# Block 0's last tile turned by a DMA on ScalarE's queue, and V of its second half made one tile at a time

## The chip, the cores and the metric

The kernel runs on one core of a Trainium2 chip. Its engines are named as the profile names them: PE (TensorE: matmuls, with PEld for its weight loads), DVE (VectorE), ACT (ScalarE), POOL (GpSimd) and SP (SyncE), which issues most DMAs; ACT has a DMA queue of its own. The metric is the device time of one execution in microseconds (us), and the plain runs are reported by their median. One more execution is taken with the hardware profiler; durations come from that one.

## The reference

Four layers work on x, 2048 tokens by 1024 columns in bf16: attention, a gated two-matrix feed-forward, and both once more with the same weights.

```python
x = A_x
x = x + _A_ref(_layernorm(x, axis=-1), A_wqkv, A_wo)
x = x + _B_ref(_layernorm(x, axis=-1), B_W_gate, B_W_up, B_W_down)
x = x + _A_ref(_layernorm(x, axis=-1), A_wqkv, A_wo)
x = x + _B_ref(_layernorm(x, axis=-1), B_W_gate, B_W_up, B_W_down)
```

`_A_ref` multiplies the normalized x with `wqkv` to Q, K and V in 32 heads of 32 columns; each token attends to itself and seven tokens 2, 4, ... 14 places earlier; the result is multiplied with `wo`. `_B_ref` is `(relu(x @ W_gate) * (x @ W_up)) @ W_down` with 3584 columns inside. `_layernorm` takes the mean off each row and divides by the root of the variance plus 1e-5.

## The kernel before

The tokens are cut into four blocks of 512 (`BLK`), and a block into four tiles of 128 rows. Eight passes (two pairs of layers times four blocks) are laid out by hand as a list of events with due times; `emit` sorts them, and so the order of the instructions on each engine is fixed. Helpers chain what they issue: `mm` and `pe_group` for PE, `dv` for DVE, `sp_dma` (line 115; the DMA issue itself is line 118 or 121) for SP's queue, and `on` (line 323) inside the first normalization for DVE, ACT ("a") and POOL ("g"). Line 132 is any matmul, line 423 a transpose on PE, line 106 any chained DVE operation, line 328 an operation of `on`.

This case is about the first 30 us, in which block 0 is normalized and multiplied with V's weights. A matmul wants the normalized x with its columns on the partitions, so every tile has to be turned: `xnT[:, t, kc, :]` is the chunk kc (of eight, 128 columns each) of tile t. In `ln_first` PE turns a tile by eight transposes into PSUM (`turn`, line 411), and ACT or DVE copies the two halves of four chunks into `xnT` (`copy`, line 426). Later blocks are turned by a DMA transpose on SP's queue.

Tiles 0 and 1 are turned without their scale, to start sooner; V of these two is scaled by `scaled(i)` (line 487) as DVE takes it out of PSUM, and `widen` (line 399) scales their part of `xnT` afterwards for Q and K. Tiles 2 and 3 are normalized fully by `apply` (line 404) before they are turned. Tile 3's statistics come from ACT (`square_of`, `act_mean`), tile 2's from DVE.

V's weights come in two slabs of four chunks each, `("v0", 0)` and `("v0", 1)`, loaded chunk by chunk in `load_slab` (line 222) with the loads of x's tiles 2 and 3 among them. V of a block has eight column groups c, and a PSUM bank (`pairs[part, c // 2]`) holds two of them for two tiles. `prod(kc, c, t0, t1)` (line 476) is one matmul of chunk kc, group c, tiles t0 to t1: 128 columns for one tile, 256 for two. `halves(i, part, k0)` (line 496) does both groups of a bank from chunk k0 on, for both tiles of the part. The order of all this is that of `head` (line 501).

Weights lie in a ring of five slabs (`RING`, line 58). The slab after the fifth, the second half of K's weights, goes into the buffer of V's first slab, so SP waits at it until PE has read that slab for the last time; behind it on SP's queue stand tiles of x for later blocks, a small zero pad of V's store, and block 1's four transposes.

```python
if (t, c) == (2, KC // 2):
    later(3)
    ln["widen"]()
```

These lines stand in `head` in the middle of tile 2's matmuls: `later(3)` turns and copies tile 3 there. After the four-chunk matmuls of tiles 2 and 3, `halves` finishes both tiles together, chunks 4 to 7.

Of the kernel before, what the change touches and what calls it, by code (L numbers as in the profile page):

```python
# [13 lines left out]
P = 128  # L14
D = 1024
# [5 lines left out]
KC = D // P  # L21
BLK = 512
TPB = BLK // P
# [8 lines left out]
def _ap(t, off, dims):  # L32
    return bass.AP(tensor=t.tensor, offset=t.offset + off, ap=[list(t.ap[0])] + [list(d) for d in dims])
# [3 lines left out]
def kernel(  # L37
# [11 lines left out]
    nc = tc.nc  # L49
# [51 lines left out]
    def dv(f, *args, **kwargs):  # L101
        if tail_dve[0] is None:
            tail_dve[0] = f(*args, **kwargs).ins
        else:
            with tc.issue_after(tail_dve[0]):
                tail_dve[0] = f(*args, **kwargs).ins  # L106
# [8 lines left out]
    def sp_dma(dst, src, transpose=False):  # L115
        start = nc.sync.dma_start_transpose if transpose else nc.sync.dma_start
        if tail_sp[0] is None:
            tail_sp[0] = start(dst, src).ins  # L118
        else:
            with tc.issue_after(tail_sp[0]):  # L120
                tail_sp[0] = start(dst, src).ins  # L121

    @contextmanager
    def pe_group():
        if tail_pe[0] is None:
            yield
        else:
            with tc.issue_after(tail_pe[0]):
                yield

    def mm(*args, **kwargs):
        tail_pe[0] = nc.tensor.matmul(*args, **kwargs).ins  # L132

    def big_tile(shape, name, early=False):
        where = pool["early"] if early else big
        return where.tile(shape, BF16, tag="big", name=name)
# [34 lines left out]
    def load_x(b, tiles=range(TPB)):  # L171
        for t in (b * TPB + i for i in tiles):
            if t == 0:
                sp_dma(x_tiles[t][:, 0:SLAB], x_dram[t * P:(t + 1) * P, 0:SLAB])
                nc.scalar.dma_start(x_tiles[t][:, SLAB:D], x_dram[t * P:(t + 1) * P, SLAB:D])
            elif t == 1:
                nc.scalar.dma_start(x_tiles[t][:], x_dram[t * P:(t + 1) * P, :])
            else:
                sp_dma(x_tiles[t][:], x_dram[t * P:(t + 1) * P, :])
# [42 lines left out]
    def load_slab(key, src):  # L222
        shp = list(src.shape)
        t = wring.tile([P, 8 * SLAB], BF16, tag="slab", name="w_" + "_".join(str(k) for k in key))
        tv = t[:, 0:shp[1] * shp[2]].rearrange("p (a b) -> p a b", b=shp[2])
        if key[0] == "v0":
            for i, (k0, k1) in enumerate(((0, 1), (1, 2), (2, 3), (3, 4)) if key[1] == 0 else ((0, 1), (1, 2), (2, 3), (3, 4))):
                if (key[1], i) in ((1, 1), (1, 2)):
                    load_x(0, [i + 1])
                sp_dma(tv[:, k0:k1, :], src[:, k0:k1, :])  # L230
        else:
            sp_dma(tv, src)
        slab[key] = tv
# [59 lines left out]
    def ln_dve_stats(xt):  # L293
# [9 lines left out]
        return mv, rstd  # L303

    load_slab(("v0", 0), qkv_half(2, 0))
    load_slab(("v0", 1), qkv_half(2, 1))
    load_slab(("qk01", "q", 0), qkv_half(0, 0))

# [8 lines left out]

    def ln_first():
        hold = {"xnT": xnT_pool.tile([P, TPB, KC, P], BF16, tag="xnT", name="xnT_first")}
        xna = big_tile([P, TPB, D], "xn_first", True)  # L320
        last = {}

        def on(eng, f, *args, **kwargs):
# [148 lines left out]
    def v_first(ln):  # L472
        st = att[0]
        pairs, opened = {}, set()

        def prod(kc, c, t0, t1):
            part = t0 // 2
            if (part, c // 2) not in pairs:
                pairs[part, c // 2] = psum.tile([P, 2, BLK // 2], F32, tag="acc", name="acc_v")
            acc = pairs[part, c // 2][:, c % 2, (t0 % 2) * P:(t0 % 2 + t1 - t0) * P]  # L480
            with pe_group():
                mm(acc, lhsT=slab["v0", kc // (KC // 2)][:, kc % (KC // 2), c * P:(c + 1) * P],
                   rhs=ln["xnT"][:, t0:t1, kc, :], start=(part, c // 2) not in opened, stop=(kc == KC - 1),
                   skip_group_check=True)
            opened.add((part, c // 2))

        def scaled(i):
            dv(nc.vector.tensor_tensor, st["vT"][:, 2 * i:2 * i + 2, 0:2 * P], pairs[0, i][:],
               _ap(ln["rb"], 0, [[0, 2], [1, 2 * P]]), op=ALU.mult)

        def later(t):
            ln["turn"](t)
            ln["copy"](t, "a", 0)
            ln["copy"](t, "a", 1)

        def halves(i, part, k0):
            for c in (2 * i, 2 * i + 1):
                for kc in range(k0, KC):
                    prod(kc, c, 2 * part, 2 * part + 2)

        def head():
            st["vT"] = big_tile([P, KC, BLK], "vT_0", True)
            ln["open_up"]()

            def chunk(kc, t):
                for c in range(KC):
                    prod(kc, c, t, t + 1)

            for kc in range(3):
                chunk(kc, 0)  # L510
            ln["turn"](1, (0,))
            ln["copy"](1, "v", 0)
            chunk(3, 0)
            ln["turn"](1, (1,))
            ln["copy"](1, "a", 1)
            ln["spread_rstd"]()
            for kc in range(4):
                chunk(kc, 1)
            chunk(4, 0)
            chunk(4, 1)  # L520
            ln["bn"](2, 0)
            ln["bn"](2, 1)
            ln["aggr"](2)
            ln["apply"](2)
            sq = ln["square_of"](x_tiles[3][:])
            ln["act_mean"](3)
            ln["act_power"](3, sq)
            chunk(5, 0)
            chunk(5, 1)
            for c in range(4):  # L530
                prod(6, c, 0, 2)
            for i in range(KC // 2):
                if i == 2:
                    later(2)
                halves(i, 0, 7 if i < 2 else 6)
                if i == 2:
                    ln["apply"](3)
                scaled(i)
            for t in (2, 3):
                for c in range(KC):  # L540
                    if (t, c) == (2, KC // 2):
                        later(3)
                        ln["widen"]()
                    for kc in range(KC // 2):
                        prod(kc, c, t, t + 1)
            for i in range(KC // 2):
                halves(i, 1, KC // 2)
                ln["on"]("a", nc.scalar.copy, st["vT"][:, 2 * i:2 * i + 2, 2 * P:BLK], pairs[1, i][:])
            tail_act[0] = ln["last"]["a"]

        return head
# [279 lines left out]
    def gu_steps(n, ln):  # L831
        hold = {}

        rs, ups = {}, {}

        def mults(j):
            def f():
                if j == 0:
                    hold["hT"] = pool["hid"].tile([P, FC, BLK], BF16, tag="hT", name=f"hT_{n}")
                s4, jl = j // 4, j % 4  # L840
                for nm in ("g", "u"):
                    acc = psum.tile([P, BLK], F32, tag="acc", name=f"acc_{nm}")
                    with pe_group():
                        for kc in range(KC):
                            mm(acc[:], lhsT=slab[(nm, n, s4)][:, kc, jl * P:(jl + 1) * P], rhs=ln["xnT"][:, :, kc, :],
                               start=(kc == 0), stop=(kc == KC - 1))
                    if nm == "g":
                        rs[j] = pool["hid"].tile([P, BLK], BF16, tag="r", name="r", bufs=3)
                        with tc.issue_after(tail_exp[0]):
                            tail_act[0] = nc.scalar.activation(rs[j][:], acc[:], ACT.Relu).ins  # L850
                    else:
                        ups[j] = acc
            return f

        def gate(j):
            def f():
                dv(nc.vector.tensor_tensor, hold["hT"][:, j, :], ups.pop(j)[:], rs.pop(j)[:], op=ALU.mult)
            return f

        return ([(2 * GRP * j, mults(j)) for j in range(FC)] + [(2 * GRP * (j + 1) - 0.05, gate(j)) for j in range(FC)],  # L860
                hold)
# [88 lines left out]
    ln_a = {}  # L950
    ln_b = {}
    ln_a[0] = ln_first()

    def zero_v():
# [36 lines left out]
    want_qk("qk23", t_qk2 + GRP * 2 * KC, t_gu0)  # L991
    want_wo(0, t_fill, t_fill)
    head = v_first(ln_a[0])
    ev.append((0.25, head))
    ev.append((0.35, lambda: load_x(1, [0, 1])))
# [53 lines left out]
    for n in range(NN):  # L1049
        gu, hold = gu_steps(n, ln_b[n])  # L1050
# [103 lines left out]
```

## Time and profile before

| | |
|---|---|
| median of three plain runs | 1616.0 us (1615.85 to 1616.05) |
| profiled execution | 1619.0 us, span 1617.3 us |
| PE busy | 1609.1 us, 99% of the span |
| DVE, ACT, POOL busy | 71%, 29%, 11% |
| PE from V's first long stretch (8.6 us) to Q's first matmul (25.0 us) | one chain without a hole |
| K weights, second half | issued at 21.56 us, after a wait of 9.6 us |

In the rows of a timeline the first column is the start in us from the span's start, the second the length; "x8" says that eight instructions of one kind are put together, and square brackets give idle time of the engine before the row and what ended it. In the chain of waits the second column is the time that the piece holds the chain. Matmuls overlap in their ends, so the length of one matmul is no price of it; prices are taken from chains of many.

### The profile page before, as it was taken

What the parts mean: (1) busy time and instruction counts of PE and PEld (TensorE: products, weight loads), DVE (VectorE), ACT (ScalarE), POOL (GpSimd) and SP (SyncE); (2) the same over time, 40 slices, a digit from 0 to 9 for tenths busy, and PEclk for the clock granted to TensorE, in tenths of its full rate; (3) what the DMA queues carried; (4) which work ended last, traced back from release to release, by engine and by line L of the source; (5) the groups of instructions that cost most, each with busy time, mean ns of one, the idle gap of its engine ahead of it and who ended that gap; (6) DMA issues with size and microseconds to landing.
All of it is one profiled execution on the core that took longest, in us unless ns stands there. A gap on an engine that the chain in (4) does not pass through costs nothing.

```text
span 1617.3 us, 19041 instructions
## 1 busy us (share of the span) xinstructions
PE 1609.1 (99%) x7651; PEld 790.5 (49%) x7701; DVE 1141.6 (71%) x969; ACT 474.8 (29%) x968; POOL 175.3 (11%) x174
## 2 busy tenths in 40 slices
PE   9999999999999999999999999999999999999999
PEld 7646544444444445444454444544445444444445
DVE  6999988997989698929489293893939939311211
ACT  4853311131116313603136031360313311131110
POOL 2400000010002002300053000530005100000000
PEclk9999999999999999999999999999999999999999
DMA  9877858586659666784757847479574884655452
GB/s 292 187 197 233 233 167 250 183 212 208 208 188 232 185 183 217 189 245 149 223 162 203 241 151 226 156 204 255 162 228 152 210 241 156 208 157 181 156 167 68
DMA packets 359561, 317.94 MB, mean 197 GB/s; under 512 B 105136, under 2 KB 333616, under 8 KB 358960
## 3 DMA queue, kind: packets, MB, share of 16 engines
q1 hardware_dynamic: 358896, 316.13, 66.7%
q8 instruction: 60, 0.98, 0.2%
q10 hardware_dynamic: 576, 0.59, 0.1%
q14 instruction: 29, 0.24, 0.0%
HBM read 266.29 MB, written 34.66 MB: 186 GB/s over the span
## 4 chain that ended last, share of the span: by engine, by line
PE 99%; DMA 0%; issue 0%; DVE 0%; SPq 0%; DVEq 0%
PE acc_u L132 24%; PE acc_g L132 24%; PE dacc L132 18%; PE acc_v L132 7%; PE acc_k L132 7%; PE acc_q L132 7%; PE acc_wo L132 7%; PE dacc_pair L132 5%; DMA w_v<-in_A_wqkv_dram 0%; DVE x L907 0%; PE tp_pair L423 0%; SPq L121 0%; PE L L132 0%; PE tp_second L423 0%; SPq L118 0%
## 5 line engine op out<-in xcount | busy, mean ns | idle before, releaser
L132 PE MATMUL acc_u<-xnT_b,w_u 128*128 128x512 bf16 x1792 | 423.5, 379 | 0.0
L132 PE MATMUL acc_g<-xnT_b,w_g 128*128 128x512 bf16 x1792 | 423.4, 379 | 0.0
L850 ACT ACTIVATE r<-acc_g 128x512 bf16<-128x512 f32 x224 | 133.6, 596 | 728.7 <-PE acc_g L132 677.8
L106 DVE TENSOR_TENSOR hT<-acc_u,r 128x512 bf16<-128x512 f32 x224 | 150.7, 686 | 240.9 <-PE acc_u L132 238.2
L132 PE MATMUL dacc<-w_d,hT 128*128 128x512 bf16 (+2 forms) x1427 | 303.5, 369 | 1.5
L132 PEld LDWEIGHTS <-hT 128*128 128x128 bf16 x1876 | 181.1, 98 | 206.2
L132 PEld LDWEIGHTS <-w_u 128*128 128x128 bf16 x1792 | 175.2, 98 | 211.6
L132 PEld LDWEIGHTS <-w_g 128*128 128x128 bf16 x1792 | 175.0, 98 | 211.7
L106 DVE TENSOR_TENSOR pv<-a,vhm 128x4096 bf16<-128x4096 bf16 x64 | 143.5, 2282 | 0.0
L907 DVE TENSOR_TENSOR x<-dacc,x 128x512 bf16<-128x512 f32 (+2 forms) x40 | 24.9, 653 | 154.3 <-PE dacc L132 154.3
L663 DVE TENSOR_TENSOR t<-q,k 128x2048 f32<-128x2048 bf16 x56 | 128.0, 2292 | 6.7 <-ACT k L598 4.6
L106 DVE TENSOR_TENSOR t<-q,k 128x2048 f32<-128x2048 bf16 x56 | 127.4, 2285 | 3.6 <-ACT k L598 2.5
L106 DVE TENSOR_TENSOR pv<-pv 128x1024 bf16<-128x1024 bf16 (+1 forms) x128 | 113.7, 948 | 0.0
L132 PE MATMUL acc_wo<-w_o,oT 128*128 128x512 bf16 x498 | 111.1, 379 | 0.7
L679 DVE TENSOR_TENSOR ac<-ac,t 128x2048 f32<-128x2048 f32 x48 | 109.6, 2284 | 0.3
L106 DVE TENSOR_TENSOR ac<-ac,t 128x2048 f32<-128x2048 f32 x48 | 109.6, 2284 | 0.0
L604 POOL COPY kh<-k 128x14 bf16<-128x14 bf16 x40 | 53.9, 1353 | 507.6 <-ACT k L598 507.6
L265 POOL TENSOR_TENSOR st_b<-st_b,neg_half 128x1 f32<-128x1 f32 x29 | 41.3, 1433 | 528.5 <-ACT st_b L264 528.5
L132 PE MATMUL dacc_pair<-w_d,hT 128*128 128x512 bf16 (+1 forms) x413 | 92.5, 372 | 0.4
L132 PEld LDWEIGHTS <-oT 128*128 128x128 bf16 x512 | 50.0, 98 | 60.4
L260 ACT ACTIVATE xn_b<-x 128x1024 bf16<-128x1024 bf16 x29 | 30.3, 1045 | 131.7 <-DVE x L106 69.5
L467 ACT CAST vT<-acc_v 128x512 bf16<-128x512 f32 x56 | 32.5, 586 | 56.7 <-PE acc_v L132 55.7
(146 smaller groups left out, 1235.4 us busy)
## 6 DMA issues: line engine op xcount, KB each, us to landing
w_g<-in_B_W_gate_dram SPq DMA_DIRECT2D x56, 1024.0 KB, 7.1
w_u<-in_B_W_up_dram SPq DMA_DIRECT2D x56, 1024.0 KB, 5.3
w_d<-in_B_W_down_dram SPq DMA_DIRECT2D x48, 1024.0 KB, 6.3
w_o<-in_A_wo_dram SPq DMA_DIRECT2D x16, 1024.0 KB, 8.2
vhm<-v_d SPq DMA_DIRECT2D x32, 284.0 KB, 6.7
v_d<-vT SPq DMA_DIRECT2D x8, 1024.0 KB, 8.9
oT<-o_d SPq DMA_DIRECT2D x32, 256.0 KB, 3.7
w_d<-in_B_W_down_dram SPq DMA_DIRECT2D x16, 512.0 KB, 3.6
```

What stands on the lines that cost most here:

```text
L106: tail_dve[0] = f(*args, **kwargs).ins
L132: tail_pe[0] = nc.tensor.matmul(*args, **kwargs).ins
L260: nc.scalar.activation(xn, xt[:], ACT.Square, accum_out=sq)
L265: nc.gpsimd.tensor_tensor(rstd, vpe, neg_half[:, 0:1], op=ALU.pow)
L467: tail_act[0] = nc.scalar.copy(st["vT"][:, c, :], acc[:]).ins
L604: nc.gpsimd.tensor_copy(khalo[n][:, c, :], k[:, BLK:BLK + HALO])
L663: nc.vector.tensor_tensor(t[:], i0, i1, op=ALU.mult)
L679: nc.vector.tensor_tensor(o, i0, i1, op=ALU.add)
L850: tail_act[0] = nc.scalar.activation(rs[j][:], acc[:], ACT.Relu).ins
L907: run = dv if n < NB - 2 else (lambda f, *args, **kwargs: f(*args, **kwargs))
```

## The change

Tile 3 of block 0 is no longer turned by PE. After ACT has copied the near half of tile 2, it issues a DMA transpose of tile 3 on its own queue (`turn_last`), and then copies the far half of tile 2. The normalization of tile 3 (`apply(3)`) stands one `scaled` earlier on DVE. V of tile 2 is made alone, first chunks 0 to 3 for all eight groups, then chunks 4 to 7, and then V of tile 3 alone, all eight chunks of a group in turn; after every second group ACT copies a finished bank. `widen` stands before these matmuls in the text; on DVE it comes after the four `scaled` as it did before. The load of x's tile 3 comes one weight chunk sooner on SP's queue.

```diff
-                if (key[1], i) in ((1, 1), (1, 2)):
-                    load_x(0, [i + 1])
+                if (key[1], i) == (1, 1):
+                    load_x(0, [2, 3])
...
-        xna = big_tile([P, TPB, D], "xn_first", True)
+        xna = hold["xn"] = big_tile([P, TPB, D], "xn_first", True)
...
+        def turn_last():
+            ln["on"]("a", nc.scalar.dma_start_transpose, ln["xnT"][:, TPB - 1, :, :], ln["xn"][:, TPB - 1, :])
...
                 if i == 2:
-                    later(2)
+                    ln["turn"](2)
+                    ln["copy"](2, "a", 0)
+                    turn_last()
+                    ln["copy"](2, "a", 1)
                 halves(i, 0, 7 if i < 2 else 6)
-                if i == 2:
+                if i == 1:
                     ln["apply"](3)
                 scaled(i)
-            for t in (2, 3):
+            ln["widen"]()
+            for kcs in (range(KC // 2), range(KC // 2, KC)):
                 for c in range(KC):
-                    if (t, c) == (2, KC // 2):
-                        later(3)
-                        ln["widen"]()
-                    for kc in range(KC // 2):
-                        prod(kc, c, t, t + 1)
-            for i in range(KC // 2):
-                halves(i, 1, KC // 2)
-                ln["on"]("a", nc.scalar.copy, st["vT"][:, 2 * i:2 * i + 2, 2 * P:BLK], pairs[1, i][:])
+                    for kc in kcs:
+                        prod(kc, c, 2, 3)
+            for c in range(KC):
+                for kc in range(KC):
+                    prod(kc, c, 3, 4)
+                if c % 2 == 1:
+                    ln["on"]("a", nc.scalar.copy, st["vT"][:, c - 1:c + 1, 2 * P:BLK], pairs[1, c // 2][:])
```

## The prediction

> **What bounds the kernel now.** I read the page first, then the chain of waits over the first 31 us, then the timelines of DVE, ACT and SP around the change, then the DMA landings and the granted clock by stretch.
>
> The page: PE has work in 1609 of 1617 us and carries 99% of the chain that ended last. A microsecond moves the end only if PE gains or loses it.
>
> ```profile
> PE 1609.1 (99%) x7651; PEld 790.5 (49%) x7701; DVE 1141.6 (71%) x969; ACT 474.8 (29%) x968; POOL 175.3 (11%) x174
> PE 99%; DMA 0%; issue 0%; DVE 0%; SPq 0%; DVEq 0%
> ```
>
> The chain around the change (start, length, what). From 8.61 us on there is no hole in it: tile 2's transposes, 24 matmuls, tile 3's transposes, 80 matmuls, then Q at 25.03.
>
> ```profile
> 16.19 0.45 PE tp_pair L423 x8
> 16.64 1.77 PE acc_v L132 x24
> 18.41 0.45 PE tp_pair L423 x8
> 18.85 6.17 PE acc_v L132 x80
> 25.03 5.18 PE acc_q L132 x24
> 30.21 0.86 PE acc_k L132 x4
> ```
>
> The timeline of DVE (start, length, what), which writes the normalized tile 3 in the row at 17.22, between the four rescalings of V, and ACT's copies out of PSUM:
>
> ```profile
> 16.01 1.29 DVE L106 TENSOR_TENSOR vT<-acc_v,rb 128x512 bf16<-128x512 f32 x2 [1.39 <-PE acc_v L132]
> 17.22 0.54 DVE L106 TENSOR_SCALAR xn_first<-x,mean,rstd 128x1024 bf16<-128x1024 bf16 x1
> ```
> ```profile
> 16.68 1.07 ACT L328 COPY xnT_first<-tp_pair 128x512 bf16<-128x512 bf16 x2 [2.31 <-PE tp_pair L423]
> ```
>
> DMA landings, one issue at a time, in us from issue: the first and second transpose of a tile of block 1 (issued at 26.8 and 30.8), then the first half of K's weights (issued at 11.27) and the second (at 21.56, after SP had waited 9.6 us for PE to free V's first slab).
>
> ```profile
> xnT_a<-xn_a SPq DMA_TRANSPOSE x1, 6.1
> ...
> xnT_a<-xn_a SPq DMA_TRANSPOSE x1, 3.2
> ...
> w_qk_k<-in_A_wqkv_dram SPq DMA_DIRECT2D x1, 1024.0 KB, 11.3
> ...
> w_qk_k<-in_A_wqkv_dram SPq DMA_DIRECT2D x1, 1024.0 KB, 5.2
> ...
> SPq L121 <- PE acc_v L132: 9.6, 1, 9.6
> ```
>
> The stretches (after the length: PE, PEld, DVE, ACT, POOL busy, then granted clock, DMA share, GB/s): the engines of the DMA are full until 19 us, and one stretch of PE ran at half clock.
>
> ```profile
> 5.36:8.77 3.41, 1.79 (x26) 1.32 (x24) 1.88 (x5) 2.18 (x5) 1.66 (x4) 1.00 0.99 365
> 8.77:12.18 3.41, 3.41 (x35) 3.41 (x34) 2.07 (x7) 0.73 (x2) 1.27 (x6) 0.50 1.05 396
> 15.59:19.01 3.42, 3.42 (x52) 3.28 (x50) 3.00 (x6) 1.19 (x3) 0.00 (x0) 1.00 1.05 385
> 19.01:22.42 3.41, 3.41 (x56) 3.30 (x54) 3.41 (x4) 0.95 (x2) 0.00 (x0) 1.00 0.45 165
> ```
>
> **The change part by part.** PE first. Two chain rows give the prices: 16 matmuls of 128 columns and 8 of 256 took 1.77 us, 48 and 32 took 6.17 us; solved, 56.9 and 107.5 ns. Removed: tile 3's eight transposes, 0.45 us. The 32 matmuls of 256 columns (3.44 us) become 64 of 128 (3.64 us), +0.20. PE's own work falls by 0.25 us. If nothing makes it wait, it passes the 8 old matmuls of tiles 0 and 1 at 17.50, the first half of tile 2 (32 x 56.9 ns) at 19.32, the second half at 21.14, tile 3 at 24.78.
>
> x3 for a weight chunk on SP's queue: x3 lands one chunk sooner (some 0.65 us, 256 KB at the 390 GB/s of those stretches), the chunk that much later. ACT's square of x3 waited 0.2 us for it, and that goes. The chunk landed at 11.3 us and PE takes it up after 14 us, so cost nothing. The new DMA shifts each later SP load to the next of eight semaphores, so SP issues four loads some 0.7 us later, behind a queue that is full until 19 us: nothing.
>
> The normalization of tile 3 goes before the second rescaling: 17.22 - 0.60 = 16.62, done at 17.16. The rescalings behind it end 0.5 us later, the second at about 17.8 and the third at 18.4; PE wants their PSUM banks at 18.4 and 18.9. Hidden, by some 0.5 us.
>
> ACT then issues the transpose at about 17.2, between its two copies of tile 2. An issue on an idle queue took SP 1.27 us (342.1 us), the two at 26.84 took 5.16, so 3.9 the first. The far copy (0.53 us) is done between 19.1 and 21.6; PE wants it at 19.32. I take 19.1, because ACT's own queue is empty; then no wait. The long end costs 2.3 us here, but most of it would be wait for tile 3 anyhow.
>
> **The landing of tile 3 is the term that decides.** Lower bound: 3.2 us as in the row with little in front, 20.4 us, before PE wants it at 21.14. Upper bound: the 6.9 us of the transpose issued at 32.7, 24.1 us. ACT's queue is not behind SP's, but runs on the same 16 DMA engines, and these still carry the first K slab, whose last share lands at 11.27 + 11.3 = 22.6. A tile's transpose alone keeps the engines 0.93 busy for 1.5 us (343.2 to 344.7), in some 64 pieces of 256 B an engine against pieces of 2 KB. Early on, x on ACT's queue and V's weights on SP's, each 256 KB, issued within 0.04 us of each other, landed after 3.6 and 3.7 us: the queues take turns. So the slowest engine finishes both works at about 22.6 + 1.2 = 23.8. I take 23.7, near the rows of 6.1 to 6.9 us. PE then waits 23.7 - 21.14 = 2.56 us.
>
> The Trainium skill, "DMA: Bandwidth & Descriptors", section on queues, rings and completion order, says that each DMA engine takes turns between the queues that have work, by packets. The early loads agree; by that rule small packets lose against large ones, and the sum would be the one taken here.
>
> Behind it everything shifts: V's first slab is freed about 0.23 us before V's end, not 3.5 us. So the second K slab is issued 3.2 us later as PE counts. Landing 5.2 us after issue, it is there 5.0 us after V's end; K wants its second half 5.18 + 0.86 = 6.04 us after: hidden, 1.0 us to spare. Behind it on SP stand x6 to x11, the zero pad, block 1's transposes and the store of V. DVE's normalizing of block 1 ends 3.2 us later against PE; DVE's idle time before its next two products (1.14 and 1.37 us) takes up 2.5, the rest of 0.7 meets 0.9 us of slack before the head sums on PE at 104.6. No wait, narrowly.
>
> Sum: 23.7 + 3.64 + 0.05 (release) - 25.03 = **+2.4 us**: -0.25 of work, +2.56 of wait, rounding. The profiled execution took 1619.0 us (span 1617.3), the median of the plain runs is 1616.0; the sum is made on the profiled times and added to the median: **1618.4 us**.
>
> **The rivals.**
> *The transpose is hidden.* If small pieces slip in between large ones with no loss, tile 3 lands by 21.1 and only the PE saving stays: 1616.0 - 0.25 = 1615.8. For it: 3.2 us after issue is a row. Against: every such row had a nearly empty DMA in front. Chance 0.25.
>
> *The clock halves behind the wait (the other side, slower).* In 5.36 to 8.77 PE had 23 matmuls (1.3 of 3.41 us) with holes of 1.33 and 0.24 us, and the next 3.41 us ran at 0.50. The new hole is twice as long; laid over the same grid of 3.41 us it splits in two, leaving some 60% of each stretch busy. If either falls under the limit, which lies above 38% busy, a stretch of 3.41 us at half clock loses 1.7 us: 1620.1, +0.25%. It decides from about 1.7 us of hole in one stretch, if the limit is half. Chance 0.22.
> The Trainium skill, "TensorE: Matmul & The Clock Gate", Part 1, puts the drop after an idle window of about 3.4 us and warns of gaps over 3 us; by that, a hole of 2.6 us costs no clock and the time is 1618.4. The trace disagrees in kind: 1.33 us was enough.
>
> *The late K slab becomes the wait.* Should it take 7.4 us, as the first Q slab did in a full queue, K waits 1.2 us more: 1619.6. Against: DMA is idle by then. Chance 0.08.
>
> **How the numbers follow.** Forecast 0.45, hidden 0.25, clock 0.22, late slab 0.08. A change under 0.2% (3.2 us) is about what a measurement of this kernel can't tell from none; forecast, hidden and late slab lie within it, and so does a small part of the clock case (short hole), while a long hole with a halved clock exceeds it. Slower 0.22, same 0.77, faster 0.01, since nothing in these 10 us could give back 3 us. The range goes from the hidden case with a little more saving, 1615.5, to the clock case with a landing at 24.1, 1620.5.
>
> **What would show it.** The transpose on ACT at about 17.2 with 1.3 us of issue, landing near 23.7; PE waiting for that DMA before tile 3's first matmul, some 2.5 us from 21.1; no wait at tile 2's second half; the second K slab issued near 27.2; Q starting near 27.4 instead of 25.03; clock 1.00 from 12.18 on; head sums not late. I am wrong if the DMA lands before 21.5, if ACT is held in the issue for much over 2 us, or if a stretch at 0.50 appears after 19 us.

## The result, and the profile after

The changed kernel takes 1623.39 us (median of six runs, 1622.30 to 1623.85), the kernel before 1615.93 beside it (six runs, 1615.81 to 1616.20). The ratio is 1.0044, with a 95% interval of 1.0034 to 1.0054: slower by 7.5 us, where 2.4 were forecast. The profiled execution of after took 1623.4 us, span 1621.7.

The chain of waits of after, around the change (start, length, what):

```profile
13.88 0.55 DVE xn_first L106
14.42 0.03 DVE vT L106
14.45 8.69 DMA xnT_first<-xn_first
23.14 0.04 issue
23.19 6.17 PE acc_v L132 x64
29.36 5.19 PE acc_q L132 x24
```

Where before had PE from end to end, after has 8.69 us of the transpose of tile 3. The 64 matmuls behind it take 6.17 us, and by the price of 56.9 ns in the prediction they should take 3.64. Q starts at 29.36.

The timeline of PE shows where it stood still (square brackets: idle before, and what ended it), and ACT's timeline shows the issue between the two copies of tile 2:

```profile
16.48 1.95 PE L132 MATMUL acc_v<-xnT_first,w_v 128*128 128x128 bf16 x32 [0.22 <-ACT xnT_first L328]
23.19 6.17 PE L132 MATMUL acc_v<-xnT_first,w_v 128*128 128x128 bf16 x64 [4.76 <-DMA xnT_first<-xn_first]
```
```profile
13.64 0.58 ACT L328 COPY xnT_first<-tp_pair 128x512 bf16<-128x512 bf16 x1 [1.41 <-PE tp_pair L423]
14.45 1.34 ACTq L328 DMA_TRANSPOSE xnT_first<-xn_first  x1
15.84 0.58 ACT L328 COPY xnT_first<-tp_pair 128x512 bf16<-128x512 bf16 x1 [1.62 <-DVE vT L106]
```

PE had done tile 2 at 18.42 and waited 4.76 us. The issue took 1.34 us, and PE waited 0.22 us for the far copy behind it.

The same time in stretches of 3.41 us (after the length: PE, PEld, DVE, ACT, POOL busy, then granted clock, DMA share, GB/s). The clock is 0.50 from 21.50 to 28.33, for most of tile 3's matmuls:

```profile
14.68:18.09 3.41, 3.19 (x58) 3.07 (x56) 3.41 (x5) 0.58 (x1) 0.00 (x0) 1.00 1.05 387
18.09:21.50 3.41, 0.33 (x6) 0.21 (x4) 2.88 (x7) 0.00 (x0) 0.55 (x1) 1.00 1.16 333
21.50:24.91 3.41, 1.72 (x17) 1.72 (x17) 1.17 (x4) 0.00 (x0) 0.78 (x1) 0.50 0.20 15
24.91:28.33 3.42, 3.42 (x35) 3.42 (x33) 0.00 (x0) 1.17 (x2) 0.00 (x0) 0.50 0.00 0
28.33:31.74 3.41, 3.41 (x30) 2.59 (x28) 0.00 (x0) 1.76 (x3) 0.00 (x0) 1.00 0.33 67
```

The DMA engines are full until 21.5 us, with what SP had issued by 9.83 and at the end with the transpose, and soon after have nothing to do. The DMA issues of after between 9 and 24 us (KB, us from issue to landing) name the last of that load, K's first slab, which landed at 9.83 + 12.8 = 22.64; the transpose landed at 23.14, half a microsecond behind it.

```profile
w_qk_k<-in_A_wqkv_dram SPq DMA_DIRECT2D x1, 1024.0 KB, 12.8
...
xnT_first<-xn_first ACTq DMA_TRANSPOSE x1, 8.7
```

**Theory.** The transpose lands when the backlog that SP issued before it has been worked off, whenever it is issued. PE is there 4.8 us earlier, and the hole then halves the clock for tile 3. **Rivals**: the transpose takes its 8 to 9 us by itself, or because it is on ACT's queue; the new order of V or the earlier load of x3 carries part of the loss; tile 3's matmuls are slow for another reason than the clock.

### The profile page after: what moved, and what is told of

It is laid out like the page before. It is cut to its first block, busy times and chain, and to the rows that moved or that the text cites. A ratio compares the mean times of both kernels' runs of the same rounds, so it can differ in the third digit from the quotient of the medians.

```text
span 1621.7 us, 19087 instructions
## 1 busy us (share of the span) xinstructions
PE 1609.5 (99%) x7675; PEld 791.8 (49%) x7725; DVE 1142.0 (70%) x969; ACT 473.8 (29%) x966; POOL 179.2 (11%) x174
## 4 chain that ended last, share of the span: by engine, by line
PE 98%; DMA 1%; DVE 0%; issue 0%; POOL 0%; ACT 0%; DVEq 0%; POOLq 0%
PE acc_u L132 24%; PE acc_g L132 24%; PE dacc L132 18%; PE acc_q L132 7%; PE acc_k L132 7%; PE acc_wo L132 7%; PE acc_v L132 6%; PE dacc_pair L132 5%; DMA xnT_first<-xn_first 1%; DMA x<-in_A_x_dram 0%; DVE bst L106 0%; DVE xn_first L106 0%; DVE x L913 0%; POOL rpair L328 0%; POOL rstd L328 0%
## 5 line engine op out<-in xcount | busy, mean ns | idle before, releaser
L132 PEld LDWEIGHTS <-w_v 128*128 128x128 bf16 x432 | 35.4, 104 | 29.0 <-issue 5.9
```

## The experiments

**The kernel before, profiled again.** No edit.

> The kernel before, unchanged, profiled again. Theory (the profiled execution that the prediction was built on was no typical one: it was 3 us longer than the plain runs, and lost them in its first 12 us): this profile takes about 1616 us, PE has no stretch at half clock around 8.8 to 12.2 us, and Q's first matmul starts near 22.2 us, not at 25.03. Rival (the profiler always costs those 3 us): again about 1619 us, a stretch at 0.50 and Q at about 25. Plain time 1615.9 by both.

Measured: 1616.17 us against 1616.26 for the kernel before beside it, and the profiled execution 1616.14, span 1614.4. Its chain, and the stretch that had run at 0.50 in the profile that the prediction used:

```profile
13.80 1.77 PE acc_v L132 x24
15.57 0.45 PE tp_pair L423 x8
16.02 6.17 PE acc_v L132 x80
22.19 5.18 PE acc_q L132 x24
```
```profile
8.77:12.18 3.41, 3.41 (x64) 3.41 (x62) 2.44 (x7) 2.09 (x4) 2.01 (x9) 1.00 1.03 384
```

Q starts at 22.19, not 25.03, and there is no half clock. In the profile used, PE had waited 1.33 us for a chunk of V's weights at 7.93, where this one waits 0.08, and the half clock behind it cost 1.7: together the 3 us between that execution (1619.0) and its plain median (1616.0). It was not a typical execution; of 25 plain runs of the kernel before on another chip one, at 1618.6, was as long, at a mean clock of 0.999 as there. Against this profile after is 7.17 us later at Q, and stays 7.2 to 7.3 later to the end.

**The new order of V alone**, in the kernel before, with tile 3 turned by PE in its old place:

```diff
-            for t in (2, 3):
+            for kcs in (range(KC // 2), range(KC // 2, KC)):
                 for c in range(KC):
-                    if (t, c) == (2, KC // 2):
+                    if (kcs[0], c) == (0, KC // 2):
                         later(3)
                         ln["widen"]()
-                    for kc in range(KC // 2):
-                        prod(kc, c, t, t + 1)
...
```

> Only the new order of V (tile 2 alone, then tile 3 alone, ACT copying each finished bank) in the kernel before; tile 3 is still turned by PE in its old place, x's tile 3 is loaded at its old place. Theory (the DMA transpose's landing is all of the loss): plus 0.20 us for 64 matmuls of 128 columns in place of 32 of 256, so 1616.1 us, no hole in PE before Q, no stretch at half clock. Rival (the order itself costs, because V's first weight slab is held to the end of tile 3 and the second K slab comes late): K waits, 1617 us or more and up to 1623.

Measured: 1616.32 against 1616.26 us. Its chain has V in one piece and Q at 22.33, 0.14 us behind the kernel before:

```profile
15.63 0.45 PE tp_pair L423 x8
16.07 6.25 PE acc_v L132 x112
22.33 5.19 PE acc_q L132 x24
```

The second K slab is issued at 22.14 instead of 18.73 here, too, and nobody waits for it. The order is not the loss.

**Work for PE in the wait: 20 and 10 matmuls on a scratch tile**, ahead of tile 3.

```diff
+            scratch(20)        # 10 in the second kernel
             for c in range(KC):
                 for kc in range(KC):
                     prod(kc, c, 3, 4)
```

> The changed kernel with 20 extra matmuls of 512 columns (on a tile of ones, into scratch that nothing reads) on PE between tile 2 and tile 3, 20 x 0.216 = 4.3 us of the 4.76 us that PE waits. They start at 18.4 and end near 22.7, before the transpose lands at 23.1. Theory (the wait is 4.8 us, and the rest of the loss is the clock, halved because PE stood still): tile 3's 64 matmuls take 3.64 us instead of 6.17, no stretch at 0.50 after them, 1623.4 - 2.5 = 1620.9 us. Rival (tile 3's matmuls are slow for another reason, such as their order or their weights): they take 6.2 us still, 1623.4 us.

> The same with 10 extra matmuls, 2.16 us, ending near 20.6: a hole of 2.6 us is left, as long as the wait that the prediction had forecast. By the changed kernel's clock records (changes at 4.43, 21.50, 28.33, a grid of 3.413 us: 18.09, 21.50, 24.91) PE is busy 73% of the stretch to 21.50 and 50% of the next. If a stretch needs more than half, the one from 24.91 runs at 0.50, tile 3 loses about 1.7 us to it, and the time is 1622.6 us. If 50% is enough, or only the whole hole counts against 3.4 us, no half clock and 1620.9 us. Should the grid lie elsewhere, the loss is between these, for one stretch at most.

Measured: 1621.14 us with 20, 1621.10 with 10 (five runs, one of them 1625.5, for which no run here has a reason). The timeline of PE with 20, then with 10:

```profile
18.51 4.48 PE L132 MATMUL scratch<-ones 128*128 128x512 bf16 x20
23.18 3.73 PE L132 MATMUL acc_v<-xnT_first,w_v 128*128 128x128 bf16 x64 [0.20 <-DMA xnT_first<-xn_first]
```
```profile
18.49 2.32 PE L132 MATMUL scratch<-ones 128*128 128x512 bf16 x10
23.09 3.73 PE L132 MATMUL acc_v<-xnT_first,w_v 128*128 128x128 bf16 x64 [2.28 <-DMA xnT_first<-xn_first]
```

The transpose lands as before; tile 3 takes 3.73 us instead of 6.17, and the time falls by 2.3. So the loss is 4.9 us of wait (what is left with 20) and 2.3 to 2.6 of clock. With 10, a hole of 2.28 us is left and the clock stays at 1.00. The grid of 3.41 us stretches lay elsewhere than in after (they began at 18.67 and 22.08), and split the hole:

```profile
18.67:22.08 3.41, 2.14 (x10) 0.88 (x9) 3.17 (x10) 0.00 (x0) 0.55 (x1) 1.00 1.21 244
22.08:25.50 3.42, 2.41 (x44) 2.41 (x44) 0.53 (x2) 1.02 (x2) 0.78 (x1) 1.00 0.06 7
```

**The issue later**, behind ACT's second copy:

```diff
                     ln["copy"](2, "a", 0)
-                    turn_last()
                     ln["copy"](2, "a", 1)
+                    turn_last()
```

> The changed kernel with ACT's issue of the transpose moved behind its second copy of tile 2, so about 2 us later, near 16.5 us instead of 14.45. Theory (the transpose lands when the 16 DMA engines have worked off what SP had issued before it, at about 22.6 us plus half a microsecond): it lands at about 23.1 to 23.3 as before, 6.6 us after its issue, and the time stays at 1623.4 (plus 0.2 at most). Rival (a transpose from ACT's queue takes 8.7 us from its issue, whatever is in front): it lands at about 25.1, 1625.4 us or more.

Measured: 1623.23 us, landed at 23.32, 8.3 us after its issue. The issue came only 0.56 us later (15.01), and that because DVE had normalized tile 3 later in this execution (at 14.98, not 14.42). In after ACT had stood at the issue for the normalization, so its second copy now comes first, at no cost. The landing moved by 0.18 us, the landing of K's first slab by 0.13. A transpose of 8.69 us from its issue would have landed at 23.70. It speaks for the theory, but the step was smaller than intended.

**x3 loaded at its old place:**

```diff
-                if (key[1], i) == (1, 1):
-                    load_x(0, [2, 3])
+                if (key[1], i) in ((1, 1), (1, 2)):
+                    load_x(0, [i + 1])
```

> The changed kernel with only the load of x's tile 3 put back to its old place on SP's queue, one weight chunk later. Theory (backlog): the normalization of tile 3 and the issue of the transpose come at most 0.7 us later, the landing stays at about 23.1 to 23.3, and the time at 1623.4 us (1622.9 to 1623.6). Rival (the earlier load of tile 3 pushes a weight chunk or the queue back, and is part of the loss): 1622.5 us or less.

Measured: 1623.21 us against 1615.99; the transpose issued at 14.72, landed at 23.00. The load is no part of the loss.

**The old order of V, with the DMA transpose** (the loops over `kcs` and c taken back to the old ones, without `later(3)`):

```diff
-            for kcs in (range(KC // 2), range(KC // 2, KC)):
+            for t in (2, 3):
                 for c in range(KC):
-                    for kc in kcs:
-                        prod(kc, c, 2, 3)
+                    for kc in range(KC // 2):
+                        prod(kc, c, t, t + 1)
...
```

> The changed kernel with the old order of V (first chunks 0 to 3 of tile 2 and of tile 3, then chunks 4 to 7 of both together, 32 matmuls of 256 columns), tile 3 still turned by the DMA on ACT's queue. Theory (the landing near 23.1 is fixed by the backlog, and the new order only gives PE 1.8 us of work to do while it waits): PE waits from about 16.6 on, 6.5 us; behind the wait 1.82 + 3.44 us of matmuls, some 2.6 us more at half clock, so Q starts near 31 instead of 22.2: 1624.9 us (1623.5 to 1626). Rival (the new order is part of the loss): 1623.4 us or less.

Measured: 1625.24 us, PE waited 7.39 us. The new order is worth 2 us here, as work for PE while it waits.

**Less in front of the transpose.** Three kernels hold loads back. In the first the transpose is issued on SP's queue between Q's two slabs, in the second behind both, in the third it stays on ACT's queue and K's first slab is issued on that queue behind it.

```diff
         def turn_last():
-            ln["on"]("a", nc.scalar.dma_start_transpose, ln["xnT"][:, TPB - 1, :, :], ln["xn"][:, TPB - 1, :])
+            sp_dma(ln["xnT"][:, TPB - 1, :, :], ln["xn"][:, TPB - 1, :], True)
...
     load_slab(("qk01", "q", 0), qkv_half(0, 0))
+    load_slab(("qk01", "q", 1), qkv_half(0, 1))    # in the second kernel only
```
```diff
             ln["on"]("a", nc.scalar.dma_start_transpose, ln["xnT"][:, TPB - 1, :, :], ln["xn"][:, TPB - 1, :])
+            load_slab(("qk01", "q", 1), qkv_half(0, 1))
+            load_slab(("qk01", "k", 0), qkv_half(1, 0), lambda dst, src: ln["on"]("a", nc.scalar.dma_start, dst, src))
...
```

> The changed kernel with the transpose of tile 3 issued on SP's queue, between the two slabs of Q's weights, so that Q's second slab, x's tiles 4 and 5 and K's first slab are only issued after it (3.5... MB less in front or beside it: of the loads that landed up to 22.6 us only those up to 15.5 us are left). Theory (backlog): issued at about 14.45, landed between 17.7 (3.2 us after issue, as with little in front) and 18.9; PE wants it at 18.4, so 0 to 0.5 us of wait and no half clock: 1615.7 to 1616.2 us, Q near 22. Q's second slab is issued near 16 and lands by about 20, before PE takes it up at 22.4. Rival (it is the transpose itself that takes 8.7 us): landed at 23.1, 1623.4 us or more. Rival (the loads held back come late instead): the transpose lands by 19, but Q or K waits, 1617 to 1620 us.

> The same with Q's second slab ahead of the transpose (it landed at 18.2 in the changed kernel), x's tiles 4 and 5 and K's first slab behind it. Theory (backlog): lands at 18.2 plus 0.5 to 1.5, so near 19.2; PE waits 0.8 us, and such a short hole leaves its stretch more than half busy, so no half clock: 1615.7 + 0.8 = 1616.5 us (1616.1 to 1617.0). Rival (the transpose itself is slow): 23.1, 1623.4 us.

> The changed kernel with K's first slab issued on ACT's queue, right behind the transpose, instead of on SP's at 9.8 us. In front of the transpose stay Q's two slabs and x's tiles 4 and 5, which had landed at 19.65 in the changed kernel. Theory (backlog, shared between the two queues): lands near 19.7 + 0.5 = 20.2 (19.5 to 20.6), PE waits 1.8 us instead of 4.8, 1615.7 + 1.8 = 1617.5 us without a half clock, 1619.2 with one stretch of it. Rival (ACT's queue is slow by itself, or the transpose is): lands near 23, 1623.4 us.

Measured: 1618.45, 1616.86 and 1618.25 us against 1616.00; no stretch at half clock behind the wait in any of them. (What the first holds back is 2.5 MB: two slabs of 1 MB and two tiles of x, not the 3.5 of its expectation.) The landings of all kernels with a DMA transpose, from the trace in us:

| kernel | issued | last load issued ahead of it landed | transpose landed | behind that load |
|---|---|---|---|---|
| after | 14.45 | 22.64 (K, first slab) | 23.14 | 0.50 |
| 20 scratch matmuls | 14.70 | 22.64 | 23.14 | 0.50 |
| 10 scratch matmuls | 14.68 | 22.49 | 23.04 | 0.55 |
| issue later | 15.01 | 22.78 | 23.32 | 0.54 |
| x3 back | 14.72 | 22.44 | 23.00 | 0.56 |
| old order of V | 14.74 | 23.36 | 23.77 | 0.41 |
| K's slab behind, ACT's queue | 14.74 | 19.12 (x, tile 5) | 20.00 | 0.88 |
| SP's queue, behind Q's slabs | 14.57 | 18.39 (Q, second slab) | 19.31 | 0.92 |
| SP's queue, Q's second slab in halves (below) | 14.58 | 16.37 (Q, first half of the second slab) | 17.75 | 1.38 |
| SP's queue, between Q's slabs | 14.54 | 15.51 (Q, first slab) | 17.75 | 2.24 |

Issued within 0.6 us of each other, the transposes land over 6 us; what they follow is the load ahead of them, with a floor of 3.2 us from the issue in the last two rows. A transpose that takes 8 us by itself is out, and so is ACT's queue as the cause.

The first of the three lands it before PE wants it, and yet loses 2.45 us: the last rival of its expectation, not the theory's 1615.7 to 1616.2. The timeline of PE shows K's two slabs as the next wait (1.86 us together), and the stretch 14 to 16 us shows why: while SP stands at the transpose, waiting for tile 3's normalization, the DMA engines run empty.

```profile
27.00 1.08 PE L132 MATMUL acc_k<-xnT_first,w_qk_k 128*128 128x512 bf16 x4 [0.23 <-DMA w_qk_k<-in_A_wqkv_dram]
29.72 0.65 PE L132 MATMUL acc_k<-xnT_first,w_qk_k 128*128 128x512 bf16 x2 [1.63 <-DMA w_qk_k<-in_A_wqkv_dram]
```
```profile
14.00:16.00 2.00, 2.00 (x36) 1.97 (x34) 2.00 (x4) 0.68 (x2) 0.00 (x0) 1.00 0.09 17
```

The second keeps a wait of 1.13 us for the transpose and loses 0.9, within its expectation (the interval of the ratio, 0.9997 to 1.0015, does not tell it from the kernel before). The third waits 0.73 us for the transpose and 0.95 for ACT's copy of tile 2, which now stands behind two issues; so the expected 1.8 us of wait came (1.68), but by two ways, and the time is 0.75 us above the 1617.5 expected for it.

**Q's second slab in two halves, the transpose between them,** to have little in front and no empty engines:

```diff
         def turn_last():
-            ln["on"]("a", nc.scalar.dma_start_transpose, ln["xnT"][:, TPB - 1, :, :], ln["xn"][:, TPB - 1, :])
+            q1 = wring.tile([P, 8 * SLAB], BF16, tag="slab", name="w_qk01_q_1")
+            q1v = q1[:].rearrange("p (a b) -> p a b", b=D)
+            sp_dma(q1v[:, 0:2, :], qkv_half(0, 1)[:, 0:2, :])
+            sp_dma(ln["xnT"][:, TPB - 1, :, :], ln["xn"][:, TPB - 1, :], True)
+            sp_dma(q1v[:, 2:4, :], qkv_half(0, 1)[:, 2:4, :])
+            slab["qk01", "q", 1] = q1v
...
```

> The changed kernel with the transpose on SP's queue in the middle of Q's second slab, which is loaded as two halves (512 KB ahead of the transpose, 512 KB behind it), so that the DMA engines have work while SP waits for the normalized tile 3, and little stands in front of the transpose. Theory (backlog, with the bubble of the transpose ahead of Q's whole second slab taken out): the first half lands near 17.0, the transpose at 17.8 to 18.5; PE waits 0 to 0.2 us; Q's second half, x's tiles 4 and 5 and K's first slab land by about 24, the second K slab by 27.4 before PE wants it at 28: 1615.8 us (1615.6 to 1616.1), at or just under the kernel before. Rival (a transpose on SP's queue makes what is behind it late in any case): K waits, 1617 to 1618.5 us.

Measured: 1617.22 us against 1615.99 (1.0008, interval 0.9999 to 1.0017). The transpose landed at 17.75 and PE did not wait for it: Q's first matmul is at 21.47, where the kernel before has it at 22.03. But then K's second slab is late, and at 102 us DVE's product for the head sums, behind late tiles of x:

```profile
28.10 1.08 PE L132 MATMUL acc_k<-xnT_first,w_qk_k 128*128 128x512 bf16 x4 [0.42 <-DMA w_qk_k<-in_A_wqkv_dram]
```
```profile
102.28 0.40 PE L132 MATMUL L<-s,sel 128*32 128x512 bf16 x4 [0.25 <-DVE s L106]
```

The gain in front is given back, and the time is the rival's (1617 to 1618.5). No version tried beats the kernel before.

## Why the prediction was wrong

*PE's own work, -0.25 us:* the +0.20 of the narrower matmuls was 0.14 (the new order alone). Right.

*x3, the normalization earlier, the issue on ACT:* right in kind. The issue took 1.34 us, not 1.27; the far copy "wanted at 19.32" came 0.22 us late, where no wait was taken. The earlier load cost nothing.

*"The landing of tile 3 is the term that decides":* the mechanism holds. The landing was bounded by K's first slab: forecast 22.6 + 1.2 = 23.8, taken 23.7; measured 22.64 + 0.50 = 23.14. Beside the transpose K's slab itself landed 0.45 us later than in the second profile of before (22.20), so against the 1.2 us stand 23.14 - 22.20 = 0.94. Measured from the issue it could not have been forecast: 8.69 us lies beyond both rows used as bounds (3.2 and 6.9).

*"PE then waits 23.7 - 21.14 = 2.56 us":* this step failed. The 21.14 is a time of the profiled execution before, in which PE was 2.8 us late by an early wait and a half clock of its own. SP's backlog was not late with it: K's first slab landed at 22.60 there, 22.20 in the second profile. In after, without that early loss, PE has done tile 2 at 18.42, and the wait is 4.76. "The sum is made on the profiled times and added to the median" is the fault in general: the two differed by 3.0 us, the text gave both numbers, and did not ask where the 3 us lay. They lay just ahead of the change, on one side of the race between PE and DMA.

*"The clock halves behind the wait", chance 0.22:* its mechanism was right, and it had to be the forecast once the hole was that long: 0.33 of 3.41 us busy in one stretch and 1.72 in the next, both followed by 0.50. It was sized at one stretch and 1.7 us; two stretches cost 6.17 - 3.64 = 2.53. Its bound for the limit was too low: it gives PE "1.3 of 3.41 us", 38%, in 5.36 to 8.77 (23 matmuls at 56.9 ns), where the row that it shows has 1.79 us, 52%. The limit lies above 52%, and the "some 60%" that the forecast left busy was closer to it than the text says. The point from which it decides, given as "about 1.7 us of hole in one stretch", is not contradicted: the hole of 2.28 us, split into 1.27 and 1.01, did nothing. So with the forecast's wait of 2.56 the forecast's clock could have held; the two errors come from one.

The sum with the measured terms: 1618.4 + (4.76 - 2.56) + 2.53 + 0.22 = 1623.35; measured 1623.39.

*The second K slab "hidden, 1.0 us to spare":* right. It was issued at 29.16, landed at 34.45, and PE took up its half at 34.54 + 0.86 = 35.40: 0.95 to spare. *"Head sums not late":* right. *The hidden transpose, chance 0.25:* not with this backlog; with the loads held back the transpose does hide, and the loads become the wait.

## What to carry to other kernels

A transfer on a second queue is not a transfer beside the first: date its landing by when what was issued ahead of it on the other queue is through (here half a microsecond behind, where that was the longer work), and compare that with the earliest time the waiting engine can be there. Before a sum is built on one profiled execution, set its time beside the plain median; a gap of 3 us has a place in the trace, and if it lies just ahead of the change, each wait for a DMA that is worked out from it is wrong by that much. Where the DMA engines are full, what is put ahead in the queue makes something else late: a step that PE does itself for 0.45 us was the cheaper one.

## What the runs showed of the hardware

**The transpose takes turns with the load, and its completions come together, behind the slowest engine.** The DMA rows of after by queue (packets, MB, share of 16 engines' time; q1 is SP's queue, q10 ACT's), first from 14.5 to 18.5 us, where the transpose has been issued and nothing of it moves, then from 19 to 20:

```profile
q1 hardware_dynamic: 804, 1.55, 104.9%
```
```profile
q1 hardware_dynamic: 167, 0.34, 87.9%
q10 hardware_dynamic: 167, 0.04, 18.9%
```

The transpose's first packet moves at 18.55, 4.1 us after the issue. It is 4.1 us in all six kernels with K's first slab in front and 2.4 with that slab behind; why it does not start at once stays open. From then on packet goes for packet, 167 of each queue in that microsecond, of 256 B here and 2 KB there. An engine has 64 of the transpose's and had, on average, 22 of the slab's left (357 in all), so the slab runs out first and the rest of the transpose follows it. So the landing follows the backlog here. By such turns a much longer backlog would not hold it to its end; no run has one. The Trainium skill, "DMA: Bandwidth & Descriptors", section on queues, rings and completion order, has each engine take turns between queues; these rows agree.

The engines had finished K's first slab one by one from 21.27 to 22.64. Of the 32 packets of 4 B that end the transpose, two to an engine, 30 move by 22.10 and the last two at 22.52, but its 16 completions all lie between 22.94 and 23.14. With the old order of V two engines were late with the slab (22.60 and 23.36, the other 14 by 21.85), and all 16 completions of the transpose lie between 23.57 and 23.77.

**What halves the clock.** Stretches of 3.41 us, PE busy in them by the windows, and the clock of the next: 0.33 us (10%), 0.50; 1.72 us (50%), 0.50; in the profile shown by the prediction 1.79 us (52%), 0.50; with 10 scratch matmuls 2.14 (63%) and 2.41 us (71%), 1.00; and at the end of the kernel with the transpose behind Q's slabs (1610.51 to 1613.92) 1.98 us (58%), 1.00. In these rows the limit lies between 52% and 58% of a stretch, and a stretch that is 87% busy or more gives the clock back. With x3 back the hole of 4.35 us emptied one stretch (19.19 to 22.61) and left the two beside it 74% and 87% busy, and only one stretch ran at 0.50; that execution took 1622.3 us. The Trainium skill, "TensorE: Matmul & The Clock Gate", Part 1, has the same free-running window and the same two states. These rows agree with both. Its drop after an idle window differs from them: a window half busy was enough.
